# One vector operation instead of two in narrowing 64-bit weights, with ScalarE's Prelu placing the sign

## The chip, the cores and the metric

The kernel runs on one core of one Trainium2 chip. The metric is the device time of one execution in microseconds (us). TensorE (PE) multiplies matrices, PEld is its weight load, VectorE is DVE, ScalarE is ACT, GpSimd is POOL; SP and ACT issue the transfers.

## What is computed

Three blocks stand one behind the other. The inputs of the kernel are 32-bit floats, except the two weights of the second block, which reach the chip as 64-bit floats.

```python
# attention over a pooled memory: batch 4, 8 heads, 576 positions, 64 wide, 32 memory slots
a      = softmax(phi, axis=positions)
k_m    = einsum('bhsm,bhsd->bhmd', a, k);  v_m = einsum('bhsm,bhsd->bhmd', a, v)
x      = softmax(q @ k_m^T / 8) @ v_m            # then 2304 tokens x 512
# first feed-forward block, d_ff = 2048
h      = x @ w_in;   x1 = (h * cos(h)) @ w_out   # w_in and w_out are 64-bit in memory
# second block, four experts of width 1024
out    = sum_e  p_e * (relu(x1 @ w1[e]) @ w2[e])
```

## The kernel before, in words

The first part, to about 150 us, holds the attention of four batches b. For each batch, `pool_exp` (L173) exponentiates phi and transposes it, `pool_kv` (L193) pools k and v on PE (L201), and `scores` (L225) makes the second softmax: PE multiplies (L239), DVE transposes blocks and takes maxima (L246, L249), POOL subtracts (L250), ACT exponentiates (L253), DVE sums and inverts (L254 to L256), POOL scales (L257), DVE transposes back (L261), and ACT and POOL split the result into a high and a low part (`split`, L87).

The first feed-forward block goes over eight shards of 256 columns of w_in and rows of w_out. `project` (L281) folds the pooled v into w_in on PE (L287), and ACT and DVE split the product (`vw`, L88 and L89). `hidden1` (L303) multiplies it with the attention weights (PE, tile `hp`), and forms h·cos(h): ACT scales (L319) and rounds (L320), DVE subtracts (L321), ACT takes the sine (L322), DVE multiplies (L323), ACT and POOL split (`gt`). `output1` (L327) multiplies with w_out (PE, tile `op`, L341's call of `mm3`, L132) and DVE adds into `acc` (L343, L345). `hp` and the projection share two PSUM buffers, so a third `hp` waits until DVE has multiplied the first one (L323). The first two shards are done batch by batch, between the attention of the batches; the six others follow, one shard at a time, to about 430 us. The second block fills the rest, to the end.

A shard of a 64-bit weight is narrowed to 32 bits by `narrow` (L107) in two pieces of 512 numbers for each of 128 partitions. A piece is loaded into a buffer `raw64` (the profile calls it `raw`; two buffers). A 64-bit number lies there as a low word and a high word. Four operations turn it into a 32-bit float:

1. L116, ACT: the high word, read as a 32-bit float, is multiplied by 2^-112 (Copy), which moves its exponent field by 112, so that the eleven exponent bits hold the 32-bit format's exponent.
2. L117, DVE: the low word is shifted right by 29 bits.
3. L118, DVE: the high word shifted left by 3 bits is or-ed with it; the sign falls off the end.
4. L121, DVE: the sign of the high word (bit 31) is or-ed in, and the result is written to the weight tile, `wi` for w_in, `wf` for w_out.

There are 2 weights, 8 shards and 2 pieces each: 32 pieces. SP issues the loads of the first three shards, ACT those of the later ones. The program's order on each engine is set by a scheduler with a timeline of its own, which reads the whole program: an edit at one place can move instructions at others. An ACT_TABLE_LOAD stands in ACT's order wherever it goes from the exponentials (L180, L253) to the sine (L322) or back; there are ten.

Of the kernel before, what the change touches and what calls it, by code (L numbers as in the profile page):

```python
# [13 lines left out]
ACTF = mybir.ActivationFunctionType  # L14
ALU = mybir.AluOpType
# [9 lines left out]
def tile_kernel(  # L25
# [13 lines left out]
    nc = tc.nc  # L39
# [67 lines left out]
    def narrow(w, src, after=None, part=None):  # L107
        n, m = w.shape[1:]
        c = 1024 // (2 * m)
        for i in range(0, n, c) if part is None else (part * c,):  # L110
            raw = cw.tile([128, c, 2 * m], U32, tag="raw64", name="raw64")
            with tc.issue_after(after.ins) if after else nullcontext():
                (nc.scalar if after else nc.sync).dma_start(out=raw, in_=src[:, i:i + c])
            lo, hi = (raw.rearrange("p a (b t) -> p a b t", t=2)[:, :, :, t] for t in range(2))
            hif = raw.bitcast(F32).rearrange("p a (b t) -> p a b t", t=2)[:, :, :, 1]
            nc.scalar.activation(out=hif, in_=hif, func=ACTF.Copy, scale=2.0 ** -112)  # L116
            nc.vector.tensor_single_scalar(lo, lo, 29, op=ALU.logical_shift_right)  # L117
            nc.vector.scalar_tensor_tensor(  # L118
                out=lo, in0=hi, scalar=3, in1=lo, op0=ALU.logical_shift_left, op1=ALU.bitwise_or
            )  # L120
            nc.vector.scalar_tensor_tensor(  # L121
                out=w[:, i:i + c].bitcast(U32),
                in0=hi,
                scalar=0x80000000,
                in1=lo,
                op0=ALU.bitwise_and,
                op1=ALU.bitwise_or,
            )

# [138 lines left out]
    def load_in(s, after=None, part=None):  # L268
        if not part:
            wi[s] = cw.tile([128, KD, FS], F32, tag="wi", name="wi")  # L270
        narrow(wi[s], w_in[s], after, part)

    def load_out(s, after=None, part=None):
        if not part:
            wf[0] = cw.tile([128, NFC, DM], F32, tag="wf", name="wf", bufs=1)
        narrow(wf[0], w_out[s], after, part)
        if part != 0:
            wo[s] = cs.tile([128, 2, NFC, DM], F32R, tag="wo", name="wo")
            split_w(wo[s], wf[0], s > 1)
# [377 lines left out]
```

## Time and profile before

| What | Value |
|---|---|
| Median of 3 runs | 1198.53 us (1197.06 to 1201.19) |
| Profiled execution, its own time | 1199.46 us |
| Its span, first to last instruction | 1197.7 us |
| Granted TensorE clock, mean | 0.977 of full speed |
| PE busy | 1154.0 us, 96% of the span |
| DVE busy | 822.7 us, 69% |
| ACT busy | 471.5 us, 39% |
| POOL busy | 519.1 us, 43% |
| Chain that ended last | PE 85%, DVE 4%, DMA 4%, POOL 3% |

The page's busy shares are averages over stages with different limits, so the stages are read one at a time; a granted clock of 1.00 is 2.4 GHz and one of 0.50 is 1.2 GHz.

### The profile page before, as it was taken

How to read it: one execution, taken by the hardware profiler on the slowest of the kernel's cores; microseconds unless marked ns; L12 is line 12 of the kernel's file. 1: busy time of each engine (PE TensorE's matmuls, PEld its weight loads, DVE VectorE, ACT ScalarE, POOL GpSimd, SP SyncE). 2: the span in 40 equal slices, each digit the busy share in tenths (PEclk: the TensorE clock that was granted, in tenths of full speed). 3: DMA queues.
4: the chain of work that ended last, by engine and by line, in shares of the span. 5: the costliest groups of instructions: out<-in, count | busy, mean ns of one | idle time of the engine just before them, and what ended most of it. 6: DMA issues, size and time to landing. Idle time of an engine off the chain costs nothing.

```text
span 1197.7 us, 19388 instructions
## 1 busy us (share of the span) xinstructions
PE 1154.0 (96%) x7786; PEld 1034.2 (86%) x7786; DVE 822.7 (69%) x1375; ACT 471.5 (39%) x786; POOL 519.1 (43%) x597
## 2 busy tenths in 40 slices
PE   6889789999999989999999999999999999999998
PEld 4477689999999888888989898988898889989897
DVE  5976858788878886666666666697666666665665
ACT  3673646666657543222322222253223222322220
POOL 2543433233336715434544454447345534544420
PEclk7599899999999989999999999999999999999999
DMA  9820102211212201111111111113111111111102
GB/s 332 288 92 21 36 1 72 67 39 38 71 38 70 71 1 53 37 36 54 53 36 36 53 54 36 36 56 129 36 39 53 52 36 53 53 37 36 54 1 79
DMA packets 38267, 72.85 MB, mean 61 GB/s; under 512 B 2561, under 2 KB 20001, under 8 KB 37665
## 3 DMA queue, kind: packets, MB, share of 16 engines
q1 hardware_dynamic: 33632, 58.99, 15.0%
q10 hardware_dynamic: 4480, 12.58, 3.2%
q8 instruction: 61, 1.00, 0.4%
q0 software_dynamic: 64, 0.04, 0.1%
q14 instruction: 30, 0.24, 0.1%
HBM read 66.88 MB, written 4.72 MB: 60 GB/s over the span
## 4 chain that ended last, share of the span: by engine, by line
PE 85%; DVE 4%; DMA 4%; POOL 3%; issue 2%; ACT 2%; POOLq 0%; ACTq 0%; DVEq 0%
PE op L132 46%; PE hp L132 36%; DMA kv<-in_kv_dram 1%; PE vw_ps L287 1%; DMA raw<-in_w_out_dram 1%; DMA raw<-in_w_in_dram 1%; PE kvp L201 1%; POOL wa L491 1%; POOL gt L89 1%; PE warm L368 1%; DMA raw<-in_w_dram 1%; DVE y L321 0%; DVE y L323 0%; DVE acc L343 0%; DVE raw L118 0%
## 5 line engine op out<-in xcount | busy, mean ns | idle before, releaser
L132 PE MATMUL op<-wb,ht 128*128 128x512 f32 x1728 | 439.9, 396 | 0.0
L132 PEld LDWEIGHTS hp<-x,wa 128*128 128x128 f32 x2688 | 380.6, 189 | 24.0 <-DVE x L448 3.5
L132 PE MATMUL hp<-x,wa 128*128 128x320 f32 (+1 forms) x2688 | 393.3, 295 | 3.1 <-DVE x L448 3.1
L132 PEld LDWEIGHTS op<-wb,ht 128*128 128x128 f32 x1728 | 313.2, 188 | 58.6
L580 DVE SCALAR_TENSOR_TENSOR acc<-op,p_all,acc 128x512 f32<-128x512 f32 x270 | 201.7, 748 | 136.9 <-PE op L132 136.7
L132 PE MATMUL op<-gt,wo 128*128 128x288 f32 x1536 | 227.2, 299 | 9.0 <-DVE acc L343 6.9
L132 PEld LDWEIGHTS op<-gt,wo 128*128 128x128 f32 x1536 | 211.1, 189 | 20.4 <-DVE acc L343 8.6
L96 POOL TENSOR_TENSOR wb<-raw,wb 128x256 fp32r<-128x256 f32 x124 | 90.0, 758 | 224.4 <-ACT wb L94 224.4
L551 ACT ACTIVATE ht<-c 128x256 fp32r<-128x256 f32 (+3 forms) x128 | 71.8, 562 | 283.4 <-DVE c L521 283.4
L89 POOL TENSOR_TENSOR gt<-y,gt 128x576 fp32r<-128x576 f32 x64 | 97.6, 1525 | 190.7 <-ACT gt L88 149.5
L552 DVE SCALAR_TENSOR_TENSOR ht<-c,ht 128x256 fp32r<-128x256 f32 (+3 forms) x128 | 94.5, 738 | 63.0 <-ACT ht L551 63.0
L491 POOL TENSOR_TENSOR wa<-raw,wa 128x256 fp32r<-128x256 f32 x96 | 69.2, 749 | 149.8 <-ACT wa L481 149.8
L132 PE MATMUL hp<-attnT,vw 128*128 128x288 f32 x768 | 119.8, 305 | 9.6 <-DVE y L323 9.6
L132 PEld LDWEIGHTS hp<-attnT,vw 128*128 128x128 f32 x768 | 110.5, 196 | 13.0 <-DVE y L323 8.4
L521 DVE TENSOR_TENSOR c<-hp,u 128x256 f32<-128x256 f32 (+1 forms) x192 | 87.3, 457 | 42.3 <-PE hp L132 37.8
L491 POOL TENSOR_TENSOR wa<-tt,wa 128x256 fp32r<-128x256 f32 x128 | 111.4, 900 | 1.2 <-ACT wa L485 1.2
L345 DVE TENSOR_TENSOR acc<-op,acc 128x576 f32<-128x576 f32 (+1 forms) x120 | 84.9, 711 | 29.4 <-PE op L132 28.2
L528 ACT COPY p<-hp 128x256 f32<-128x256 f32 x64 | 25.5, 399 | 112.9 <-PE hp L132 112.9
L321 DVE SCALAR_TENSOR_TENSOR y<-kk,y 128x576 f32<-128x576 f32 x64 | 55.0, 859 | 15.1 <-ACT kk L320 14.7
L319 ACT ACTIVATE y<-hp 128x576 f32<-128x576 f32 x64 | 41.4, 647 | 47.1 <-PE hp L132 40.1
L481 ACT ACTIVATE wa<-raw 128x512 fp32r<-128x512 f32 x32 | 20.2, 632 | 87.5 <-PE hp L132 85.3
L323 DVE TENSOR_TENSOR y<-hp,y 128x576 f32<-128x576 f32 x64 | 48.0, 750 | 9.1 <-ACT y L322 8.4
(89 smaller groups left out, 914.6 us busy)
## 6 DMA issues: line engine op xcount, KB each, us to landing
raw<-in_w_dram SPq DMA_DIRECT2D x60, 512.0 KB, 3.5
kv<-in_kv_dram SPq DMA_DIRECT2D x16, 512.0 KB, 5.3
raw<-in_w_in_dram ACTq DMA_DIRECT2D x10, 512.0 KB, 3.3
raw<-in_w_out_dram ACTq DMA_DIRECT2D x10, 512.0 KB, 3.3
q<-in_qt_dram SPq DMA_DIRECT2D x4, 1152.0 KB, 8.0
out_dram<-acc SPq DMA_DIRECT2D x18, 256.0 KB, 2.0
raw<-in_w_in_dram SPq DMA_DIRECT2D x6, 512.0 KB, 5.4
raw<-in_w_out_dram SPq DMA_DIRECT2D x6, 512.0 KB, 4.9
```

Source lines behind the costliest of these rows:

```text
L89: (eng or nc.vector).tensor_tensor(out=lo, in0=src, in1=f32(hi), op=ALU.subtract)
L96: (nc.vector if early and c % 512 else nc.gpsimd).tensor_tensor(out=t[:, 1, c:c + 256], in0=src[:, c:c + 256], in1=f32(t[:, 0, c:c + 256]) ...
L132: nc.tensor.matmul(out=ps, lhsT=lt(a), rhs=rt(b), start=first and i == 0, stop=last and i == 2, skip_group_check=more,)
L319: marks.append(nc.scalar.activation(out=y, in_=hv, func=ACTF.Copy, scale=INV_2PI, bias=0.25))
L321: nc.vector.scalar_tensor_tensor(out=y, in0=kk, scalar=ROUND, in1=y, op0=ALU.subtract, op1=ALU.subtract)
L323: nc.vector.tensor_tensor(out=y, in0=hv, in1=y, op=ALU.mult)
L345: nc.vector.tensor_tensor(out=dst, in0=op[:, :, :TH], in1=dst, op=ALU.add)
L491: pool.tensor_tensor(out=wa[:, 1, o], in0=src, in1=f32(wa[:, 0, o]), op=ALU.subtract)
L521: nc.vector.tensor_tensor(out=out, in0=ps[:, :n], in1=sb, op=ALU.add)
L551: nc.scalar.activation(out=ht[:, 0, fc, lo:], in_=c[:, fc, lo:], func=ACTF.Relu)
L552: nc.vector.scalar_tensor_tensor(out=ht[:, 1, fc, lo:], in0=c[:, fc, lo:], scalar=0.0, in1=f32(ht[:, 0, fc, lo:]), op0=ALU.max, op1=ALU.su ...
L580: nc.vector.scalar_tensor_tensor(out=dst, in0=op, scalar=pe, in1=dst, op0=ALU.mult, op1=ALU.add)
```

## The change

ACT's function in L116 becomes Prelu: a positive number is multiplied by 2^-112 as before, a negative one by 2^-112 and then by alpha = 2^32. The second factor adds 32 to the field of eight exponent bits that a 32-bit read sees, which is 256 in the eleven bits of the 64-bit exponent: bit 28 of the high word is set for a negative number and clear for a positive one. After the shift left by 3, bit 28 is bit 31, the sign of a 32-bit float. So the operation of L118 already gives the finished weight. It now writes the weight tile, and that of L121 is gone; one DVE instruction of two operands less for each of the 32 pieces. Lines behind `narrow` have numbers lower by 3 in the changed kernel, and L118 now writes `wi` and `wf`.

```diff
-            nc.scalar.activation(out=hif, in_=hif, func=ACTF.Copy, scale=2.0 ** -112)
+            nc.scalar.activation(out=hif, in_=hif, func=ACTF.Prelu, scale=2.0 ** -112, alpha=2.0 ** 32)
             nc.vector.tensor_single_scalar(lo, lo, 29, op=ALU.logical_shift_right)
-            nc.vector.scalar_tensor_tensor(
-                out=lo, in0=hi, scalar=3, in1=lo, op0=ALU.logical_shift_left, op1=ALU.bitwise_or
-            )
             nc.vector.scalar_tensor_tensor(
                 out=w[:, i:i + c].bitcast(U32),
                 in0=hi,
-                scalar=0x80000000,
+                scalar=3,
                 in1=lo,
-                op0=ALU.bitwise_and,
+                op0=ALU.logical_shift_left,
                 op1=ALU.bitwise_or,
             )
```

The scheduler answers with another order at many places of the first part. Three are shown.

**Place one, DVE, the second shard's weights** (`raw_219` and `raw_214` are the second piece of w_in, `raw_375` and `raw_369` the first of w_out). Before:

```order
L117 TENSOR_SCALAR raw_219<-raw_219 128x512
L177 TENSOR_SCALAR nmx<-nmx 128x1
L118 SCALAR_TENSOR_TENSOR raw_219<-raw_219 128x512
L121 SCALAR_TENSOR_TENSOR wi<-raw_219 128x512
L246 STREAM_TRANSPOSE st<-sc 128x288 x2
L249 TENSOR_REDUCE smx<-st 128x18
L117 TENSOR_SCALAR raw_375<-raw_375 128x512
L118 SCALAR_TENSOR_TENSOR raw_375<-raw_375 128x512
L121 SCALAR_TENSOR_TENSOR wf<-raw_375 128x512
L89 TENSOR_TENSOR vw<-vw_ps,vw 128x1024
```

Changed:

```order
L117 TENSOR_SCALAR raw_214<-raw_214 128x512
L118 SCALAR_TENSOR_TENSOR wi<-raw_214 128x512
L243 STREAM_TRANSPOSE st<-sc 128x288 x2
L117 TENSOR_SCALAR raw_369<-raw_369 128x512
L246 TENSOR_REDUCE smx<-st 128x18
L118 SCALAR_TENSOR_TENSOR wf<-raw_369 128x512
L89 TENSOR_TENSOR vw<-vw_ps,vw 128x1024
```

Two operations of two operands are gone ahead of the split of `vw`, one in each piece.

**Place two, ACT, the second attention batch** (`st` is the second softmax, `y` the sine's tile, `kvs` the pooled k and v, `ex` the exponential of phi). Before:

```order
L88 ACTIVATE gt<-y 128x576
L209 ACTIVATE kvs<-kvp,rs 128x256
L322 ACTIVATE y<-y 128x576
L180 ACT_TABLE_LOAD
L180 ACTIVATE ex,rs<-phi,nmx 128x576
L253 ACTIVATE st<-st 128x576
```

Changed:

```order
L88 ACTIVATE gt<-y 128x576
L250 ACT_TABLE_LOAD
L250 ACTIVATE st<-st 128x576
L319 ACT_TABLE_LOAD
L319 ACTIVATE y<-y 128x576
L206 ACTIVATE kvs<-kvp,rs 128x256
L177 ACT_TABLE_LOAD
L177 ACTIVATE ex,rs<-phi,nmx 128x576
```

The softmax has moved ahead of the sine, which takes two more table loads; `kvs` stands behind both. The whole program has 12 table loads now and had 10, and none of them stands at L116.

**Place three, PE and ACT, where the last attention batch begins** (`sc` is the scores' product, `vw_ps` the projection, `raw_1681`, `raw_1687`, `raw_1671` and `raw_1676` are w_out of the third shard). PE before:

```order
L287 MATMUL vw_ps<-wi,vT 32x256 x15
L239 MATMUL sc<-q,kT 32x288 x4
L287 MATMUL vw_ps<-wi,vT 32x256
L132 MATMUL op<-gt,wo 128x288 x6
L132 MATMUL hp<-attnT,vw 128x288 x12
L132 MATMUL op<-gt,wo 128x288 x42
```

PE, changed:

```order
L236 MATMUL sc<-q,kT 32x288 x8
L284 MATMUL vw_ps<-wi,vT 32x256 x16
L129 MATMUL op<-gt,wo 128x288 x18
L129 MATMUL hp<-attnT,vw 128x288 x12
L129 MATMUL op<-gt,wo 128x288 x30
```

ACT at the same place, before:

```order
L322 ACTIVATE y<-y 128x576
L88 ACTIVATE vw<-vw_ps 128x1024
L253 ACT_TABLE_LOAD
L253 ACTIVATE st<-st 128x576
L88 ACTIVATE gt<-y 128x576
L116 ACTIVATE raw_1681<-raw_1681 128x512
L319 ACTIVATE y<-hp 128x576
L320 ACTIVATE kk<-y 128x576
L116 ACTIVATE raw_1687<-raw_1687 128x512
L253 ACTIVATE st<-st 128x576
L322 ACT_TABLE_LOAD
L322 ACTIVATE y<-y 128x576
```

ACT, changed:

```order
L250 ACT_TABLE_LOAD
L250 ACTIVATE st<-st 128x576
L88 ACTIVATE vw<-vw_ps 128x1024
L250 ACTIVATE st<-st 128x576
L319 ACT_TABLE_LOAD
L319 ACTIVATE y<-y 128x576
L116 ACTIVATE raw_1671<-raw_1671 128x512
L116 ACTIVATE raw_1676<-raw_1676 128x512
L316 ACTIVATE y<-hp 128x576
```

On PE, 18 products `op` instead of 6 stand ahead of the twelve `hp`; on ACT the sine that these twelve wait for has moved behind both softmaxes and both table loads.

## Rows read from the trace of the kernel before

**Rows 1.** The profile page: busy time by engine, and the granted clock in 40 slices.
```profile
PE 1154.0 (96%) x7786; PEld 1034.2 (86%) x7786; DVE 822.7 (69%) x1375; ACT 471.5 (39%) x786; POOL 519.1 (43%) x597
...
PEclk7599899999999989999999999999999999999999
```

**Rows 2.** Busy time by stage: stretch, length, engines, granted clock, DMA share, GB/s.
```profile
0.00:150.00 150.00, 120.13 (x1082) 91.55 (x1083) 109.23 (x232) 82.26 (x128) 58.72 (x57) 0.85 0.45 153
150.00:430.00 280.00, 273.15 (x2292) 261.78 (x2290) 218.37 (x304) 174.94 (x264) 117.13 (x95) 0.99 0.16 50
430.00:1197.70 767.70, 760.72 (x4416) 680.91 (x4414) 495.09 (x841) 214.30 (x395) 343.25 (x446) 1.00 0.15 47
```

**Rows 3.** DVE groups by form, 0 to 150 us: busy, mean ns, idle before.
```profile
L118 DVE SCALAR_TENSOR_TENSOR raw<-raw 128x512 uint32<-128x512 uint32 x12 | 11.3, 951 | 0.2
...
L121 DVE SCALAR_TENSOR_TENSOR wi<-raw 128x512 uint32<-128x512 uint32 x6 | 5.5, 932 | 0.0
...
L121 DVE SCALAR_TENSOR_TENSOR wf<-raw 128x512 uint32<-128x512 uint32 x6 | 4.1, 676 | 0.0
```

**Rows 4.** DVE groups by form, 165 to 430 us.
```profile
L118 DVE SCALAR_TENSOR_TENSOR raw<-raw 128x512 uint32<-128x512 uint32 x20 | 13.6, 681 | 0.0
```

**Rows 5.** ACT groups by form, whole execution.
```profile
L116 ACT ACTIVATE raw<-raw 128x512 f32<-128x512 f32 x32 | 22.2, 693 | 27.6 <-DMA raw<-in_w_in_dram 15.0 <-DMA raw<-in_w_out_dram 12.6
...
L551 ACT ACTIVATE ht<-c 128x512 fp32r<-128x512 f32 x32 | 20.2, 632 | 105.8 <-DVE c L521 105.8
...
L180 ACT ACTIVATE ex<-phi,nmx 128x576 f32<-128x576 f32 x8 | 6.2, 772 | 2.2 <-DVE nmx L177 2.1
```

**Rows 6.** Timeline of DVE, 46 to 50 us: start, duration, instruction.
```profile
46.54 1.46 DVE L118 SCALAR_TENSOR_TENSOR raw<-raw 128x512 uint32<-128x512 uint32 x1
48.04 0.69 DVE L121 SCALAR_TENSOR_TENSOR wf<-raw 128x512 uint32<-128x512 uint32 x1
48.65 1.22 DVE L89 TENSOR_TENSOR vw<-vw_ps,vw 128x1024 fp32r<-128x1024 f32 x1
```

**Rows 7.** Timeline of ACT, 45 to 47 us.
```profile
45.76 1.02 ACT L88 ACTIVATE vw<-vw_ps 128x1024 fp32r<-128x1024 f32 x1 [0.23 <-PE vw_ps L287]
```

**Rows 8.** Timeline of PE, 48 to 60 us.
```profile
49.92 5.31 PE L132 MATMUL hp<-attnT,vw 128*128 128x288 f32 x22
...
59.25 1.08 PE L201 MATMUL kvp<-kv,es 128*32 128x128 f32 x32 [1.44 <-ACT es L187]
```

**Rows 9.** Timeline of ACT, 61 to 65 us; in brackets the idle time before.
```profile
61.06 0.46 ACT L209 ACTIVATE kvs<-kvp,rs 128x256 f32<-128x256 f32 x1
62.16 0.69 ACT L322 ACTIVATE y<-y 128x576 f32<-128x576 f32 x1 [0.65 <-DVE y L321]
62.87 1.28 ACT L180 ACT_TABLE_LOAD   x1
64.16 0.78 ACT L180 ACTIVATE ex<-phi,nmx 128x576 f32<-128x576 f32 x1
```

**Rows 10.** Timeline of DVE, 60 to 66 us.
```profile
62.05 1.91 DVE L118 SCALAR_TENSOR_TENSOR raw<-raw 128x512 uint32<-128x512 uint32 x1
```

**Rows 11.** Timeline of PE, 124 to 165 us.
```profile
133.23 3.25 PE L132 MATMUL hp<-attnT,vw 128*128 128x288 f32 x12 [3.50 <-DVE y L323]
...
141.75 1.86 PE L132 MATMUL op<-gt,wo 128*128 128x288 f32 x12 [1.89 <-DVE acc L343]
145.09 1.06 PE L132 MATMUL op<-gt,wo 128*128 128x288 f32 x6 [1.48 <-DVE acc L343]
...
160.90 3.18 PE L132 MATMUL hp<-attnT,vw 128*128 128x288 f32 x12 [3.11 <-DVE y L323]
```

**Rows 12.** Busy time of 5 us stretches, columns as in rows 2.
```profile
140.00:145.00 5.00, 1.86 (x12) 1.62 (x12) 5.00 (x12) 2.03 (x4) 1.91 (x2) 1.00 0.00 0
145.00:150.00 5.00, 4.62 (x22) 4.39 (x23) 1.87 (x6) 1.10 (x2) 3.39 (x4) 0.68 0.00 0
```

**Rows 13.** Timeline of DVE, 139 to 144 us.
```profile
139.26 1.29 DVE L118 SCALAR_TENSOR_TENSOR raw<-raw 128x512 uint32<-128x512 uint32 x2
...
141.98 0.68 DVE L121 SCALAR_TENSOR_TENSOR wf<-raw 128x512 uint32<-128x512 uint32 x1
```

## The prediction

> **What bounds the kernel now.** The page comes first: PE is busy for 1154.0 us of a span of 1197.7, DVE for 822.7, and the granted clock is below full in a few early slices only [rows 1]. A saving on DVE is worth nothing where PE is full, so the next view is the busy time by stage. From 150 us on PE is busy for 273.15 of 280 us and then for 760.72 of 767.70 [rows 2]: it is the limit there, and DVE has 62 and 273 us of idle time. In the first 150 us PE is busy for 120.13 only, at a mean granted clock of 0.85. That stretch alone can give time back: 29.9 us in which PE stands, and what it loses at half clock.
>
> Which wait ends last in it? At 133.23 PE has stood 3.50 us for the product of the sine (DVE, L323), at 141.75 and 145.09 for 1.89 and 1.48 us until DVE had emptied a PSUM buffer (L343), at 160.90 again 3.11 us for L323 [rows 11]. DVE is busy for all of 140 to 145 us [rows 12]. Before, from about 20 to 55 us, transfers, DVE, ACT and a PE at 1.2 GHz take turns [rows 1].
>
> **The change part by part.** *The removed operation.* One DVE instruction goes for each of 32 pieces. Undisturbed it takes 0.68 us, as L118's twenty of the later stage show [rows 4]. Twenty pieces lie behind 150 us, where PE is the limit: 20 x 0.68 = 13.6 us of DVE time that I cost at nothing, since PE's queue covers them; without that cover it would be all 13.6. Twelve pieces lie in the first 150 us, where L118 and L121 have means of 951, 932 and 676 ns [rows 3]: between 12 x 0.68 = 8.2 and 12 x 0.95 = 11.4 us are removed there. What is longer than 0.68 us runs beside POOL's operations; I take it as a wait for POOL that the next DVE operation would meet, and so as not saved. The Trainium skill, page "SBUF — State Buffer", section "Who interferes with whom", says that a DVE instruction with two SBUF inputs and a GpSimd instruction that reads SBUF exclude one another for a whole instruction; by that rule, too, the removal is worth 8.2 and not 11.4 us, and no row here shows which of the two POOL instructions held the port.
>
> How much of the 8.2 us is on the path? The first four pieces go before 35 us, where PE waits for k and v from memory or works at half clock, and DVE itself waits for the next weights: nothing. At place one the order shows what counts. ACT has the high part of `vw` ready at 45.76 + 1.02 = 46.78 us [rows 7]; DVE begins the low part at 48.65 only, since L118 (1.46 us) and L121 (0.69 us) of another piece stand in front [rows 6], and PE begins its 22 products at 49.92 [rows 8]. With two operations fewer ahead of it, `vw` can start when ACT is done: at most 48.65 - 46.78 = 1.9 us, at least the 0.69 us of the operation that stood last. Next late is `es` on ACT, for which PE waits until 59.25 [rows 8]; behind the first sine it still has the same operations in front. **I take 1.2 us gained**, nearer to what ACT allows than to nothing, and 0 to 1.9 as its ends.
>
> *Place two.* The order has two table loads more on ACT, both in front of `kvs`. One load takes 1.28 us, 62.87 to 64.15, and the exponential follows at 64.16 [rows 9], so two cost 2.6 us of ACT. Against it stand the 0.65 us that ACT idles before the sine [rows 9], and the L118 of 1.91 us at 62.05, which held DVE just then [rows 10] and leaves this place. PE has twelve products `op` to do meanwhile. The loss lies between 2.6 us, if nothing covers the loads, and 2.6 - 0.65 - 1.91 = 0.0 us, if both do; the products on PE make it nearer to the second. **I take 0.5 us lost.** The Trainium skill, page "ScalarE: Activation LUTs", section "What ACT_TABLE_LOAD costs", gives 1283 ns for a load and some 1380 ns of drain, 2.66 us for each switch. By that two switches would take 5.3 us instead of 2.6. The load agrees with the trace; the drain does not show, since the sine ends at 62.85, the load begins at 62.87, and its successor at 64.16 [rows 9].
>
> *Place three.* On PE 18 products `op` instead of 6 stand ahead of the `hp` that waits for L323. Twelve products take 1.86 us [rows 11], so 1.9 us of the 3.50 us wait can be filled. Against it, ACT now runs two softmaxes, `vw` and two loads ahead of the sine. Behind it DVE loses two operations, 2 x 0.68 = 1.4 us, from a stretch in which it is busy without a gap [rows 12] and PE waits 1.89 and 1.48 us for it; the removed ones are one of L118 and L121 in each of the two pieces at 139 to 144 us [rows 13]. The softmax of the last batch is also ready earlier. The gain has 3.4 us as its upper end (both waits of [rows 11] on L343) and -1.0 as its lower one (the sine's delay wins over the filled wait). **I take 2.6 us gained**, because DVE's full stretch is what ends last there.
>
> *Prelu for Copy.* No row shows a Prelu. On 512 numbers Copy takes 693 ns here and Relu 632; the exponential, on 576 and with a bias from memory, takes 772 [rows 5]. I take 0.69; the ends, 632 and 772, change 32 pieces by -2 and +2.5 us of an ACT that is never the limit for that long, so nothing comes of it.
>
> *The sum:* -1.2 + 0.5 - 2.6 = -3.3 us. The profiled execution's own time is 1199.46 us (its span 1197.7 and 1.8 around it), which gives 1196.2. It lies 0.93 us above the median of 1198.53, so for a median **I forecast 1195.2 us**. With the ends of the three terms the case runs from 1198.5 - 1.9 - 0.0 - 3.4 = 1193.2 to 1198.5 + 0.0 + 2.6 + 1.0 = 1202.1.
>
> **The rivals.** *All of the removed time reaches the end.* The first part is then bound by DVE throughout: 8.2 us gained, 1190.3 us. For it speaks that DVE is full around 140 us [rows 12]; against it that DVE waits for weights before 35 us and that its busy time in the first part is 109.23 of 150 us [rows 2].
>
> *The sine comes late (slower).* At place three the sine for the waiting `hp` now stands behind load, softmax, `vw`, softmax and load: 1.28 + 0.69 + 1.02 + 0.69 + 1.28 = 5.0 us by [rows 7, 9], the softmaxes taken as long as a sine. The 1.9 us of products cover part, and 3.1 us remain. The wait of 3.50 us grows, and another group of twelve runs at 1.2 GHz, as at 160.90, where it takes 3.18 instead of 1.86 us [rows 11]: 1.3 us. With place two at its price uncovered, 2.6, and 1.2 gained at place one, this is 1198.5 + 5.8 = 1204.3 us. It decides if the sine ends more than the 1.9 + 1.4 us of the gains later than before. For it speaks the fall of the clock to 0.68 in 145 to 150 us [rows 12], which shows how near PE is to half clock there; against it that the softmaxes that came first were themselves awaited.
>
> *It is hidden.* PE's order and the transfers set the first part, and the new order only changes which wait is seen: 1198.5 us. For it speaks that PE is at half clock where most of the twelve pieces lie [rows 1].
>
> **How the numbers follow.** A measurement of this kernel tells a difference from none at about 0.3%, 3.6 us: faster means below 1194.9, slower above 1202.1. My forecast has 0.58, and by its ends 0.24 of that lies below 1194.9 and 0.34 within. All removed time has 0.16, the late sine 0.16, nothing 0.10. So faster 0.24 + 0.16 = 0.40, same 0.34 + 0.10 = 0.44, slower 0.16. The range goes from 1189.8, which takes in the first rival, to 1201.0, near my case's upper end, where all three terms would have to be at their worst; it leaves out the late sine and little else, under 0.2.
>
> **What would show it.** In the changed profile L121 is gone, L118 stands 32 times at 0.68 us and more, and DVE's busy time is 22 to 30 us less (32 x 0.68 to 32 x 0.95). ACT has 12 loads. PE's 22 products begin near 48.7 us; `kvs` of the second batch is late by one to two microseconds; PE's waits for L343 around 140 us shrink; behind 165 us PE is as full as before, only some 3 us earlier. I am wrong if PE's wait for L323 near 133 us has grown beyond 5 us, if a further stretch near 60 or 130 us is at half clock, or if L116 is slower than 0.8 us.

## The result, and the profile after

| | before | after |
|---|---|---|
| median of 8 runs | 1198.30 us | 1204.71 us |
| lowest to highest | 1196.39 to 1201.19 | 1203.10 to 1207.78 |
| profiled execution, own time | 1199.46 us | 1203.10 us |
| its span | 1197.7 us | 1201.3 us |

The ratio is 1.0053, with a 95% interval from 1.0038 to 1.0068: the change made the kernel slower by half a per cent, 6.4 us. The profiled execution of after is the lowest of its eight, so its trace shows 3.6 us of span and not the whole difference.

The page of after, busy time by engine, the granted clock and one group of products (in the changed kernel all lines behind the narrowing are 3 lower: L132 is now L129, L345 is L342):

```profile
PE 1150.8 (96%) x7786; PEld 1031.5 (86%) x7786; DVE 806.9 (67%) x1343; ACT 472.8 (39%) x788; POOL 513.0 (43%) x597
...
PEclk7699899999999999999999999999999999999999
...
L129 PE MATMUL op<-gt,wo 128*128 128x288 f32 x1536 | 228.4, 300 | 16.3 <-DVE acc L342 9.5
```

Against [rows 1] DVE has 32 instructions and 15.8 us of work less, and PE has as many products as before in a longer span. The slices below full clock are still the early ones (a slice is 30 us long). The last line names what is new: 9.5 us in which products `op` of the first stage stood for `acc`.

The removed operation and its neighbours in the whole execution of after, as groups on DVE and on ACT:

```profile
L118 DVE SCALAR_TENSOR_TENSOR wi<-raw 128x512 uint32<-128x512 uint32 x16 | 12.8, 804 | 0.5 <-ACT raw L116 0.4
...
L118 DVE SCALAR_TENSOR_TENSOR wf<-raw 128x512 uint32<-128x512 uint32 x16 | 10.8, 674 | 0.0
...
L116 ACT ACTIVATE raw<-raw 128x512 f32<-128x512 f32 x32 | 22.1, 690 | 29.6 <-DMA raw<-in_w_in_dram 17.4 <-DMA raw<-in_w_out_dram 12.2
```

One shift-or writes each weight, and ACT's scaling takes 690 ns as Prelu against 693 as Copy [rows 5]. The operation itself does what it should.

Busy time by stage, the stretches and columns of [rows 2]:

```profile
0.00:150.00 150.00, 121.54 (x1100) 93.85 (x1101) 97.81 (x221) 84.96 (x130) 59.08 (x57) 0.85 0.45 154
150.00:430.00 280.00, 266.55 (x2244) 254.93 (x2243) 211.47 (x279) 169.98 (x258) 110.46 (x94) 0.99 0.15 50
430.00:1201.30 771.30, 762.68 (x4447) 682.75 (x4445) 497.57 (x844) 217.83 (x402) 343.46 (x447) 1.00 0.15 46
```

The stage that was full is no longer so: from 150 to 430 us PE works 266.55 us instead of 273.15, and its clock is as high as before. DVE gave up 11.4 us in the first 150 us and 6.9 us here.

**The same work, not the same time.** Fixed stretches compare different work once one kernel is ahead. The projections `vw_ps` make better marks, since each kernel has 16 of them in the same order. The timeline of PE in before shows the fifth and the sixteenth:

```profile
167.20 1.09 PE L287 MATMUL vw_ps<-wi,vT 64*32 64x256 f32 x32
...
395.60 1.09 PE L287 MATMUL vw_ps<-wi,vT 64*32 64x256 f32 x32
```

and in after the same two:

```profile
162.21 1.09 PE L284 MATMUL vw_ps<-wi,vT 64*32 64x256 f32 x32
...
399.81 1.09 PE L284 MATMUL vw_ps<-wi,vT 64*32 64x256 f32 x32
```

After begins the fifth 4.99 us earlier and the sixteenth 4.21 us later. So it gains 5.0 us in the first part and loses 9.2 us between the two marks (237.60 us instead of 228.40). These are single executions; the table of the experiments shows how far two executions of one order lie apart. From the sixteenth to the end of the span it is 1197.7 - 395.60 = 802.1 us in before and 1201.3 - 399.81 = 801.5 in after: next to nothing happens there.

Between the marks the instructions stand in nearly the same order in both traces. Behind the first few microseconds PE's order is the same. On ACT five instructions have moved, the copy L94 of `w_out`, one in each shard. On POOL two subtractions L96 stand ahead of one more `gt` in each shard. On DVE the operations of L121 are gone, and in each shard one `y` and one `acc` have gone behind the two L96.

**Where the 9 us are.** The waits of PE between 165 and 430 us in after (what waits, for whom, us in total, times, longest):

```profile
PE op L129 <- DVE acc L342: 9.5, 5, 2.6
PE hp L129 <- DVE y L320: 1.4, 2, 1.0
PE op L129 <- POOL gt L89: 0.6, 1, 0.6
```

and in before, in the same stretch:

```profile
PE op L132 <- POOL gt L89: 1.8, 4, 0.9
PE hp L132 <- DVE y L323: 1.7, 2, 1.1
```

Five waits for `acc` are new, one in each of the five shards whose weights are narrowed in this stage. The one near 244 us, in the timelines of ACT, DVE, POOL and PE of after:

```profile
239.07 1.06 ACT L94 ACTIVATE wo<-wf 128x1024 fp32r<-128x1024 f32 x1
240.04 0.67 ACT L317 ACTIVATE kk<-y 128x576 f32<-128x576 f32 x1
...
238.36 0.68 DVE L118 SCALAR_TENSOR_TENSOR wf<-raw 128x512 uint32<-128x512 uint32 x1
...
239.63 0.75 DVE L342 TENSOR_TENSOR acc<-op,acc 128x576 f32<-128x576 f32 x1
240.29 1.83 DVE L96 TENSOR_TENSOR wo<-wf,wo 128x256 fp32r<-128x256 f32 x2
242.04 1.97 DVE L318 SCALAR_TENSOR_TENSOR y<-kk,y 128x576 f32<-128x576 f32 x1
243.93 0.75 DVE L342 TENSOR_TENSOR acc<-op,acc 128x576 f32<-128x576 f32 x1
...
241.80 1.60 POOL L89 TENSOR_TENSOR gt<-y,gt 128x576 fp32r<-128x576 f32 x1
...
244.73 4.70 PE L129 MATMUL op<-gt,wo 128*128 128x288 f32 x23 [1.93 <-DVE acc L342]
```

The second piece of `wf` is complete one DVE operation earlier than it was. With that, the split of `w_out` into a high and a low part is ready earlier, and the order of the program now takes it at once (why the scheduler does so is my reading: its own timeline is not recorded): ACT's copy L94 ahead of `kk`, and DVE's two subtractions L96 ahead of `y` and of the `acc` that empties PE's buffer. Between two `acc` additions DVE now does 1.83 + 1.97 us of other work. PE's next `op` needs the buffer and stands for 1.93 us. Behind that wait the granted clock is 0.57 from 246 to 250 us, where before has 1.00; the 23 products take 4.70 us there. So the 9.2 us between the marks are 8.0 us more of idle time on PE (10.0 us instead of 2.0) and 1.2 us more of busy time (227.6 instead of 226.4).

In before the same place reads, on DVE:

```profile
243.66 0.67 DVE L121 SCALAR_TENSOR_TENSOR wf<-raw 128x512 uint32<-128x512 uint32 x1
244.26 0.74 DVE L321 SCALAR_TENSOR_TENSOR y<-kk,y 128x576 f32<-128x576 f32 x1
244.94 1.41 DVE L345 TENSOR_TENSOR acc<-op,acc 128x576 f32<-128x576 f32 x2
246.27 0.74 DVE L96 TENSOR_TENSOR wo<-wf,wo 128x256 fp32r<-128x256 f32 x2
```

There both `acc` came ahead of L96, which nobody was waiting for: the shard that uses this `wo` comes later. The two L96 take 0.74 us there; the 1.83 us in after run beside POOL's two L96 (240.21 to 241.84).

The `y` of 1.97 us takes 0.74 in before. It begins beside POOL's `gt` (241.80 to 243.40) and ends 0.61 us behind it, as if it had been let in only when `gt` was done. The Trainium skill, page "SBUF — State Buffer", section "Who interferes with whom", says this of a DVE instruction with two inputs in SBUF and a GpSimd instruction that reads SBUF: the one that comes second waits for the whole of the first. This row agrees with it.

### The profile page after: what moved, and what is told of

Read it like the earlier page. It is cut to its first block, busy times and chain, and to the rows that moved or that the text cites. A ratio compares the mean times of both kernels' runs of the same rounds, so it can differ in the third digit from the quotient of the medians.

```text
span 1201.3 us, 19353 instructions
## 1 busy us (share of the span) xinstructions
PE 1150.8 (96%) x7786; PEld 1031.5 (86%) x7786; DVE 806.9 (67%) x1343; ACT 472.8 (39%) x788; POOL 513.0 (43%) x597
## 4 chain that ended last, share of the span: by engine, by line
PE 79%; DVE 3%; DMA 2%; POOL 1%; issue 1%; ACT 0%; ACTq 0%; POOLq 0%; DVEq 0%
PE op L129 44%; PE hp L129 34%; DMA raw<-in_w_out_dram 1%; DVE y L318 1%; PE vw_ps L284 1%; DVE x L445 1%; DVE acc L342 1%; DVE wo L96 1%; POOL wa L488 0%; DMA raw<-in_w_in_dram 0%; DMA raw<-in_w_dram 0%; POOL gt L89 0%; POOL wb L96 0%; DVE y L320 0%; POOL tt L477 0%
## 5 line engine op out<-in xcount | busy, mean ns | idle before, releaser
L129 PE MATMUL op<-wb,ht 128*128 128x512 f32 x1728 | 439.8, 395 | 0.0
L129 PEld LDWEIGHTS hp<-x,wa 128*128 128x128 f32 x2688 | 379.1, 188 | 26.3 <-DVE x L445 4.6
L129 PE MATMUL hp<-x,wa 128*128 128x320 f32 (+1 forms) x2688 | 392.1, 294 | 4.8 <-DVE x L445 3.9
L129 PEld LDWEIGHTS op<-wb,ht 128*128 128x128 f32 x1728 | 312.5, 188 | 58.0
L129 PE MATMUL op<-gt,wo 128*128 128x288 f32 x1536 | 228.4, 300 | 16.3 <-DVE acc L342 9.5
L129 PEld LDWEIGHTS op<-gt,wo 128*128 128x128 f32 x1536 | 212.3, 191 | 27.5 <-DVE acc L342 11.0
L96 POOL TENSOR_TENSOR wb<-raw,wb 128x256 fp32r<-128x256 f32 x124 | 90.1, 758 | 226.2 <-ACT wb L94 226.2
L89 POOL TENSOR_TENSOR gt<-y,gt 128x576 fp32r<-128x576 f32 x64 | 95.1, 1485 | 187.1 <-ACT gt L88 123.9
L129 PE MATMUL hp<-attnT,vw 128*128 128x288 f32 x768 | 118.4, 303 | 6.0 <-DVE y L320 4.8
L129 PEld LDWEIGHTS hp<-attnT,vw 128*128 128x128 f32 x768 | 109.2, 194 | 9.6 <-DVE y L320 5.0
L342 DVE TENSOR_TENSOR acc<-op,acc 128x576 f32<-128x576 f32 (+1 forms) x120 | 85.4, 712 | 30.9 <-PE op L129 30.0
L318 DVE SCALAR_TENSOR_TENSOR y<-kk,y 128x576 f32<-128x576 f32 x64 | 64.0, 1000 | 21.0 <-ACT kk L317 20.0
L319 ACT ACTIVATE y<-y 128x576 f32<-128x576 f32 x64 | 43.7, 683 | 35.2 <-DVE y L318 35.0
```

Source lines behind the costliest of these rows:

```text
L89: (eng or nc.vector).tensor_tensor(out=lo, in0=src, in1=f32(hi), op=ALU.subtract)
L96: (nc.vector if early and c % 512 else nc.gpsimd).tensor_tensor(out=t[:, 1, c:c + 256], in0=src[:, c:c + 256], in1=f32(t[:, 0, c:c + 256]) ...
L129: nc.tensor.matmul(out=ps, lhsT=lt(a), rhs=rt(b), start=first and i == 0, stop=last and i == 2, skip_group_check=more,)
L318: nc.vector.scalar_tensor_tensor(out=y, in0=kk, scalar=ROUND, in1=y, op0=ALU.subtract, op1=ALU.subtract)
L319: nc.scalar.activation(out=y, in_=y, func=ACTF.Sin, scale=-TWO_PI)
L342: nc.vector.tensor_tensor(out=dst, in0=op[:, :, :TH], in1=dst, op=ALU.add)
```

## The experiments

**Theory T** after this reading: the first part gains 5 us; the later shards lose because the split of `w_out` is taken ahead of `kk`, `y` and `acc`. **Rivals:** R1, Prelu itself costs it; R2, the first part loses (two more table loads, half clock) and the later waits follow from that; R3, DVE's subtractions are slow beside POOL wherever they stand, so that order does not matter.

All times below are medians; the ratios are to the kernel before on the same chip, with 95% intervals. The marks are those of above, the starts of the fifth and of the sixteenth projection in the profiled execution.

| kernel | median us | ratio to before | fifth begins | fifth to sixteenth |
|---|---|---|---|---|
| before | 1198.30 (after), 1198.52 (e1 to e4), 1199.50 (e5 to e8) | | 167.20 | 228.4 |
| after | 1204.71 | 1.0053 (1.0038 to 1.0068) | 162.21 | 237.6 |
| e1, short form early only | 1194.45 | 0.9961 (0.9947 to 0.9975) | 164.14 | 227.9 |
| e2, short form late only | 1209.82 | 1.0088 (1.0063 to 1.0113) | 169.03 | 236.3 |
| e3, after, split held | 1195.36 | 0.9968 (0.9956 to 0.9981) | 162.29 | 229.1 |
| e4, after, Copy for Prelu | 1204.44 | 1.0053 (1.0033 to 1.0072) | 164.37 | 236.8 |
| e5, after, DVE's part held | 1196.49 | 0.9981 (0.9963 to 0.9999) | 160.05 | 229.8 |
| e6, after, split on POOL | 1203.87 | 1.0035 (1.0021 to 1.0048) | 161.95 | 236.2 |
| e7, short form in shard 2 only | 1194.04 | 0.9955 (0.9936 to 0.9974) | 162.89 | 228.0 |
| e8, short form in shards 0 and 1 only | 1198.53 | 0.9994 (0.9981 to 1.0006) | 166.95 | 227.2 |

The median of e2 is one of 4 runs, that of e4 one of 5, that of e6 one of 9; the others have 8 to 10 and before 8, 20 and 30. From the sixteenth to the end of the span it is 801.5 to 802.9 us in all ten. The kernels fall into two groups in the last column, near 227 to 230 and near 236 to 238, and into two in the column before it, 160 to 165 and 167 to 169.

The column of the fifth also shows the spread of a single trace. Up to this mark after and e1, e3, e4, e5 and e6 have the same instructions in the same order on PE, DVE, ACT and POOL, and yet it begins at 160.05 to 164.37. Before and e2 share the other order, with 167.20 and 169.03. So in the first part one trace of each shows nothing below about 4 us; there the medians count. Between the marks the spread is smaller: with the order of before, 228.4 and 227.9 (e1), with that of after, 237.6, 236.3 (e2) and 236.8 (e4).

### e1 and e2: the change in halves

```diff
-            nc.scalar.activation(out=hif, in_=hif, func=ACTF.Prelu, ...)
-            ...
+            if after is None:
+                ...
+            else:
+                ...
```

`after` is None for the twelve pieces of the first three shards. In e1 the first branch is the short form and the second the four operations of before; in e2 the other way round.

> The short narrowing is kept for the twelve pieces of the first three shards and the four-operation form is put back for the twenty pieces behind 165 us. Theory T (the first part gains 5 us, the later shards lose because the split of w_out is taken ahead of kk, y and acc): 1193.5 us (1192 to 1195.5), no wait of the op products for acc (now L129 <- L342, 9.5 us) between 165 and 430 us. Rival R1 (Prelu itself is the cost): the twelve early ones cost their share, 3/8 of 6.4 us, so 1200 to 1201. Rival R2 (the first part loses, by table loads and half clock): 1204 or more.

> The reverse: the four-operation form for the first twelve pieces, the short one for the later twenty. Theory T: 1198.3 - 2 (waits of before that go) + 9.5 (acc waits) + 1.7 (430 to 505 us) = 1207.5 us (1205 to 1209), with 8 to 11 us of waits of op for acc between 165 and 430 us. Rival R1 (Prelu): 5/8 of 6.4 us, 1202 to 1203, no such waits needed. Rival R2 (first part): 1198 to 1199.

Measured: 1194.45 and 1209.82 us. e1 is within T's range, e2 0.8 us above it; both are far from R1 and R2: half of the change gains 4 us, the other half loses 11. One term of T for e2, 1.7 us between 430 and 505 us, did not come (802.1 us from the sixteenth to the end, as in before), so its sum is near by luck in part. Between the marks e2 loses 7.9 us. The waits of PE from 165 to 430 us in e1:

```profile
PE op L144 <- POOL gt L89: 1.6, 4, 0.6
PE hp L144 <- DVE y L335: 1.3, 2, 1.0
...
PE op L144 <- DVE acc L357: 0.2, 1, 0.2
```

and in e2:

```profile
PE op L144 <- DVE acc L357: 9.0, 5, 2.1
...
```

So the five waits come with the short form of the later twenty pieces, whatever stands in the first part. R2 is out.

### e3: the same operations, in the old order

```diff
-            split_w(wo[s], wf[0], s > 1)
+            with tc.issue_after(gts[-1].ins) if after else nullcontext():
+                split_w(wo[s], wf[0], s > 1)
```

`gts` collects ACT's copies of `gt`; the split is kept behind the last of them, which is where before had it. No operation is added or taken away. In each of the five shards one copy of `gt` on ACT also stands one place earlier, and one product `op` on PE with it; more moves at the end of the last.

> The changed kernel, but in the five later shards the split of w_out is held on ACT behind the gt copy after which the kernel before had it; every other instruction is kept. Theory T: the waits of op for acc go (9.5 us to under 3), 1196 us (1194 to 1198), faster than both kernels. Rival R1 (Prelu): 1204.7, unchanged. Rival R2 (first part): 1204.7. Rival R3 (DVE's subtractions of the split are slow beside POOL wherever they stand, so the order does not matter): waits of 7 us or more remain, 1202 to 1205.

Measured: 1195.36 us, faster than both kernels. The waits of PE from 165 to 430 us:

```profile
PE hp L130 <- DVE y L323: 2.8, 3, 1.6
PE op L130 <- POOL gt L89: 1.3, 3, 0.8
PE hp L130 <- DVE x L448: 1.2, 1, 1.2
```

No `acc` among them, and the two marks are 229.1 us apart instead of 237.6. R3 falls, too. On DVE, the groups of `y` and of the split in this stretch of e3

```profile
L321 DVE SCALAR_TENSOR_TENSOR y<-kk,y 128x576 f32<-128x576 f32 x49 | 48.7, 993 | 15.4 <-ACT kk L320 14.6
...
L97 DVE TENSOR_TENSOR wo<-wf,wo 128x256 fp32r<-128x256 f32 x12 | 9.9, 861 | 0.0
```

and in after

```profile
L318 DVE SCALAR_TENSOR_TENSOR y<-kk,y 128x576 f32<-128x576 f32 x49 | 50.7, 1035 | 15.4 <-ACT kk L317 14.5
...
L96 DVE TENSOR_TENSOR wo<-wf,wo 128x256 fp32r<-128x256 f32 x12 | 10.3, 898 | 0.0
```

are nearly as slow in the fast kernel as in the slow one. What differs is who is waiting behind them.

### e4: Prelu or the order

```diff
-            nc.scalar.activation(out=hif, in_=hif, func=ACTF.Prelu, scale=2.0 ** -112, alpha=2.0 ** 32)
+            nc.scalar.activation(out=hif, in_=hif, func=ACTF.Copy, scale=2.0 ** -112)
```

> The changed kernel with Copy in the place of Prelu and nothing else, so that the order on every engine stays that of the changed kernel; the sign of the weights of the first stage is then not moved into the exponent, and this part of the narrowing is left out. Theory T, R2: 1204.7 us (1203 to 1207), since the order is what costs. Rival R1 (Prelu): 1198 or less.

Measured: 1204.44 us, as after. On ACT the group of the scaling reads:

```profile
L116 ACT ACTIVATE raw<-raw 128x512 f32<-128x512 f32 x32 | 22.1, 691 | 27.4 <-DMA raw<-in_w_in_dram 17.9 <-DMA raw<-in_w_out_dram 9.5
```

691 ns with Copy, 690 with Prelu, and the order on PE, DVE, ACT and POOL is that of after, instruction by instruction. R1 is out.

### e5 and e6: ACT's copy or DVE's subtractions

In e5 the edit keeps back DVE's two subtractions only; ACT's copy of `w_out` (L94 of after) stays ahead of `kk`. As in e3, one `gt` on ACT and one `op` on PE stand a place earlier in each shard:

```diff
+            if held:
+                with tc.issue_after(accs[-1].ins):
+                    for f in held:
+                        f()
+                held.clear()
```

`held` has the two subtractions of the split, `accs` the additions to `acc`; the lines stand behind `output1`. In e6 POOL does all four subtractions:

```diff
-            split_w(wo[s], wf[0], s > 1)
+            split_w(wo[s], wf[0], s > 1 and after is None)
```

> The changed kernel, with ACT's early copy of w_out (ahead of kk) left where it is; only DVE's two subtractions of the split are held, behind the acc addition that they were ahead of, in the five later shards. Theory T1 (DVE's subtractions ahead of y and acc are what costs): waits of op for acc between 165 and 430 us fall from 9.5 to under 3 us, 1196 us (1194 to 1198). Theory T2 (ACT's copy of 1.06 us ahead of kk is what costs, by making y and so acc late): five waits of about 1 us stay, 1200 to 1202. If both are needed in part, between the two.

> The changed kernel with the whole subtraction of the w_out split on POOL in the five later shards, so that DVE has none of it; ACT's copy stays ahead of kk. T1: the waits for acc go, but POOL's four subtractions (about 0.85 us each, 3.4 us) may stand ahead of a gt: waits for acc under 2 us, for gt 1 to 5 us, 1195 to 1199. T2: five waits of about 1 us for acc stay, 1200 to 1203.

Measured: e5 1196.49 us, within T1's range and outside T2's. Its timeline of DVE at the place of above:

```profile
236.32 0.74 DVE L354 TENSOR_TENSOR acc<-op,acc 128x576 f32<-128x576 f32 x1
237.50 0.76 DVE L330 SCALAR_TENSOR_TENSOR y<-kk,y 128x576 f32<-128x576 f32 x1 [0.44 <-ACT kk L329]
238.19 0.75 DVE L354 TENSOR_TENSOR acc<-op,acc 128x576 f32<-128x576 f32 x1
238.85 2.00 DVE L98 TENSOR_TENSOR wo<-wf,wo 128x256 fp32r<-128x256 f32 x2
```

From one `acc` to the start of the next it is now 238.19 - 236.32 = 1.87 us, where after has 243.93 - 239.63 = 4.30. POOL's two L96 are as early as in after. ACT's early copy is seen as DVE's 0.44 us of waiting for `kk`, which PE does not feel. So, the few moves beside it apart, it is DVE's subtractions: 1.83 us by themselves, and by pushing `y` beside POOL's `gt` another 1.2 (1.97 instead of 0.76).

e6 missed: 1203.87 us, where T1 had 1195 to 1199 and T2 up to 1203. The waits for `acc` are gone (0.2 us), yet the marks are 236.2 us apart. The groups of PE between the marks, in e6:

```profile
L129 PE MATMUL op<-gt,wo 128*128 128x288 f32 x1057 | 153.0, 296 | 3.8 <-POOL gt L89 3.4 <-DVE acc L342 0.2
L129 PE MATMUL hp<-attnT,vw 128*128 128x288 f32 x528 | 78.9, 296 | 1.9 <-DVE vw L89 1.9
L284 PE MATMUL vw_ps<-wi,vT 64*32 64x256 f32 x353 | 14.9, 382 | 0.6 <-DVE y L320 0.4
```

and in e1, which has the order of before there:

```profile
L144 PE MATMUL op<-gt,wo 128*128 128x288 f32 x1057 | 153.2, 297 | 1.2 <-POOL gt L89 0.9 <-DVE acc L357 0.2
L144 PE MATMUL hp<-attnT,vw 128*128 128x288 f32 x528 | 77.2, 295 | 0.3 <-DVE y L335 0.3
L299 PE MATMUL vw_ps<-wi,vT 64*32 64x256 f32 x353 | 12.4, 382 | 0.0
```

The products are the same in number and in mean duration, but the program's order on PE is another one: 2.5 us more of busy time for `vw_ps`, 1.7 for `hp`. In four of the projections between the marks of e6, the one at 223.08 for instance, 30 products run together and the last two alone, behind twelve `op`, where the two take 0.62 us: four times that is the 2.5 us. With 3.8 + 1.9 + 0.6 us of waits instead of 1.2 + 0.3 this makes up the loss. e6 thus does not tell T1 from T2; e5 does. It shows a second time that taking operations from DVE can move others on PE, and cost more than it saves.

### e7 and e8: where the first part gains

The short form by shard instead of by stage, `short` being `s == 2` in e7 and `s < 2` in e8:

```diff
-    def narrow(w, src, after=None, part=None):
+    def narrow(w, src, after=None, part=None, short=False):
...
+            if short:
+                ...
+            else:
+                ...
```

> The short narrowing for the four pieces of the third shard alone (taken between 126 and 144 us), the four-operation form for all others. Theory P3 (all that the first part gains is gained between the projections that end near 128.5 and 163 us): that stretch is 35 us instead of 40, 1194 us (1192.5 to 1196). Theory P (by the prediction's places, 2.6 of it there and 0.7 before): 37 us, 1196.

> The short narrowing for the eight pieces of the first two shards alone (in the first 50 us), the four-operation form for all others. Theory P3: nothing is gained, 1198.5 us (1197 to 1200), the stretch between the projections near 128.5 and 168 us stays 40 us long. Theory P: 0.7 us is gained, 1197.8, and the projection that ends near 128.5 us comes 0.7 us earlier. Half-clock theory (two more table loads on ACT ahead of kvs cost up to 2.6): 1199 to 1201.

Measured: 1194.04 and 1198.53 us. The four pieces of shard 2 alone give as much as all twelve of the first part do (0.9955, and 0.9961 in e1), and the eight before them nothing that shows. e8's interval, 0.9981 to 1.0006, has room for theory P's 0.7 us, for P3's nothing and for the lower end of the half-clock theory, so e8 does not tell P3 from P. e7 does, narrowly: P's 1196 us would be 0.998 of before, just outside its interval (0.9936 to 0.9974).

The place is less clear than the sum. From the end of the fourth projection to the end of the fifth e7 takes 35.0 us (129.01 to 163.98), as P3 says. In e8 it is 36.3 us, where P3 has 40 and before 39.8: its fourth ends at 131.74, 3.2 us later than in before (128.54), and the stretch behind it is shorter. The six kernels that share an order up to the fifth mark begin the fourth anywhere from 126.32 to 129.70 us, so most of the 3.2 us can be the spread of one trace. e8 has the new order of place three, too, with both softmaxes ahead of the sine, and the long form in shard 2. There PE waits later on:

```profile
148.18 1.81 PE L144 MATMUL op<-gt,wo 128*128 128x288 f32 x6 [3.84 <-DVE acc L355]
```

In after the waits between 140 and 150 us are 0.72 and 1.11 us. That speaks for DVE's removed operations in shard 2, but no run has the order of e7 with the long form, so what the operations give and what the order gives is not told apart.

## Why the prediction was wrong

I forecast 1195.2 us, within 1189.8 to 1201.0, and gave slower a chance of 0.16, by another mechanism than the one that came. Point by point:

- **The step that failed** is "Twenty pieces lie behind 150 us, where PE is the limit: 20 x 0.68 = 13.6 us of DVE time that I cost at nothing, since PE's queue covers them". The time is covered; the order is not. In five shards the operations that went let the split of `w_out` pass `kk`, `y` and `acc`, and PE waited 9.5 us for `acc`. In its place stands +9.2 us between the marks (237.6 - 228.4), of which e3 takes back 8.5 with no operation changed. The order of ACT and DVE shows these moves without a run; the section on the change and the prediction looked at the order of the first part only, and the prediction priced the later stage by its busy time. Its two ends for this term were nothing and a gain; that it could be a loss had no end at all.
- **The first part** was forecast at -3.3 us and measured at -5.0 in the profiled execution; e1, which is that part alone, has -4.1 us by its medians. The sum was right to within its ends, the places were not, so that it came near is in part luck. Place one: `vw`'s low part began 0.75 us earlier (47.90 instead of 48.65), but the 22 products at 49.76 instead of 49.92, behind other products in PE's order. They ended 1.5 us earlier (53.77 instead of 55.23), with a granted clock of 0.84 from 50 to 55 us instead of 0.53. Place two: the two loads are there, 1283 ns each, and PE's wait moved from `es` on ACT (1.44 us) to `es` on DVE (2.97 us until 58.51, in the trace of after). From 60 to 65 us the clock is at half (rows below), and what place one gave is gone: the twelve `hp` that begin at 60.62 in before and take 1.85 us begin at 61.90 and take 3.25. e8 says what the first two shards are worth together: nothing that a measurement can tell (0.9981 to 1.0006). Place three, taken as -2.6, is all of it that shows: 0.9955 in e7, 5.4 us, with 3.1 and 7.7 as the interval's ends.
- At place three the reason given was half right. The four waits of [rows 11] become, on PE in after:

```profile
133.35 1.66 PE L129 MATMUL op<-gt,wo 128*128 128x288 f32 x6 [3.14 <-DVE acc L340]
...
141.74 1.07 PE L129 MATMUL op<-gt,wo 128*128 128x288 f32 x6 [0.72 <-DVE acc L340]
...
143.92 0.90 PE L129 MATMUL hp<-attnT,vw 128*128 128x288 f32 x2 [1.11 <-ACT attnT L88]
...
156.90 1.82 PE L129 MATMUL hp<-attnT,vw 128*128 128x288 f32 x12 [1.61 <-DVE y L320]
```

  The wait near 133 us did not shrink by the products put ahead of it; it changed from `y` to `acc` and lost 0.4 us of 3.50. The two waits for `acc` (1.89 and 1.48) fell to 0.72 and one of 1.11 for `attnT`, less than the 3.4 us that the upper end had. The fourth, 3.11 us at 160.90, halved, and its twelve products ran at full clock, 1.82 us instead of 3.18: that is what the sum had not counted.
- **Prelu** at nothing: right (690 ns; e4).
- **The signs to look for.** L121 gone, L118 32 times, 12 loads: right. DVE less by 22 to 30 us: 15.8. The narrowing itself has 29.4 us less (L118 and L121 53.0, now L118 23.6), but `y` (L318) became slower beside POOL, 1000 ns in the mean of 64 instead of 859, which is 9.0 us, and the subtractions L96 of `wo` 898 instead of 594, which is 3.6. The 22 products near 48.7 us: wrong, 49.76. `kvs` late by one to two us: 3.8 (64.90 instead of 61.06). The waits for L343 around 140 us shrink: right. One of the three signs of being wrong did come, a further stretch near 60 us at half clock. In before and in after, the columns of [rows 2]:

```profile
60.00:65.00 5.00, 4.24 (x55) 2.95 (x46) 4.63 (x5) 4.24 (x8) 3.41 (x3) 1.00 0.84 283
```

```profile
60.00:65.00 5.00, 5.00 (x49) 4.17 (x42) 2.29 (x4) 4.62 (x6) 2.65 (x2) 0.50 0.44 138
```

  It is not what made the kernel slow: e3 and e5 have 0.59 in this stretch and are faster than before; e2, with the order of before up to there, has 0.66. "Behind 165 us PE is as full as before": wrong, and that is the sign that decided.
- **The rivals.** The late sine did not come: near 133 us the clock (0.86 from 130 to 135 us, 0.82 in before) and the wait (3.14 us, 3.50 in before) are no worse. "All of the removed time reaches the end" and "hidden" both stop at nothing lost in the later stage, as the forecast did. None of the four cases had the later stage in it.

## What to carry to other kernels

Where a scheduler sets the order, a removed operation does two things: it frees time, and it changes which operation is ready first. The second is priced at the engine's neighbours: for each place in which the order moved, ask who is waiting behind the instruction that came forward, also where the engine that loses work has idle time. Here the repair is one edge in the order that keeps a piece of work nobody needs yet behind what the limiting engine does need (e3, 0.32% faster than before); or the short form only where DVE was late (e7, 0.45%).

To compare two kernels of which one is ahead, measure between the same pieces of work, not between the same times, and look for two kernels that share an order to see how far one trace varies.

## What was not expected of the hardware

- Removing four operations of 0.68 us a shard from an engine that is idle for a fifth of the stage cost 1.8 us in each of the five shards (9.2 / 5), by the order that came with it.
- DVE's `y` takes 0.74 to 0.76 us alone and up to 1.97 beside POOL's `gt` (in all five shards 1.95 to 1.97); it ends 0.61 us behind `gt`. So its price depends on when it starts, and moving two short operations ahead of it costs more than their own time.
- The projections keep PE busy for 14.9 us between the marks in e6 and for 12.4 in e1, with a mean of 382 ns in both: how they lie among other products counts, not how long one takes. Two of them alone take 0.62 us where 32 together take 1.09.
